# Three moves in a fused attention, mixture-of-experts and channel-mix kernel: when one expert's rows are loaded, where weight words are decoded, and where they are checked

## The chip, the core and the metric

The kernel runs on one core of a Trainium2 chip. TensorE (PE) does the matmuls, VectorE (DVE), ScalarE (ACT) and GpSimd (POOL) the rest, each working through its own list of instructions in order; SyncE (SP) issues most loads. Sixteen DMA engines move data between HBM and the on-chip memory. The metric is the device time of one execution in microseconds (us), as the median of several runs.

## The reference, cut to what matters

Three stages follow each other on 2 x 768 tokens of width 512. The second and third are

```python
# attention output x, (2, 768, 512), goes into
for b in range(B):
    for s in range(S):
        e = fresh_e if s == 0 or local_gate[b, s] < 0.5 else prev_e   # one of 8 experts
        h = np.maximum(x[b, s] @ w1[e], 0.0)                            # 512 -> 1024
        out[b, s] = p[e] * (h @ w2[e])                                  # 1024 -> 512
...
x_prev = np.concatenate([np.zeros((B, 1, D)), x[:, :-1, :]], axis=1)
xk = mu_k * x + (1.0 - mu_k) * x_prev
xr = mu_r * x + (1.0 - mu_r) * x_prev
k = np.maximum(xk @ w_k, 0.0)          # w_k (512, 1024), float64 in memory
v = k * k @ w_v                        # w_v (1024, 512), float64 in memory
r = 1.0 / (1.0 + np.exp(-(xr @ w_r)))  # w_r (512, 512), float64 in memory
return r * v
```

The three matrices of the last stage arrive as 64-bit numbers, so each is a pair of 32-bit words on the chip.

## The kernel before

**Matmuls in three.** Each float32 product is three matmuls (`mm3`, L608 to L610): every operand is split into a rounded "hi" part, made by an ACT copy, and a "lo" rest, made by a subtraction on DVE. So each tile of weights (512 KB) is loaded into one of four `wraw` buffers by SP, turned into `whi` by ACT (L596, two halves) and into `wlo` by DVE (L605). The buffer is free when `wlo` is made; `w_lo_all` is followed by `pump`, which issues the next load of the queue `lq` on SP. Activations go the same way (`xh`/`xl`, `hh`/`hl`, `ehh`/`ehl`).

**Stages by time.** Attention and routing take about 0 to 136 us; the routing sorts the tokens by expert into a DRAM table `xs`. Experts are then worked by rank `r`, most tokens first. The rank 0 expert is done in part while routing ends (its steps are called `fill` steps), and its third tile of 128 rows follows from about 155 to 171 us (`xs_tile`). A branch `tc.If(more > 0)` comes next, whose body isn't run with this data. Then r=1 with three tiles of rows (171 to 206 us), r=2 (206 to 230), r=3 (230 to 246), r=4 (246 to 269), r=5 (269 to 285), r=6 (285 to 310) and r=7 (310 to 333). Ranks 3 and 5 have one tile of 128 rows and are done in the form of `xs_tile`: first layer into `hn`, four transposes of `hn` on PE (L614), split into `ehh`/`ehl`, second layer. Ranks 1, 2, 4 and 6 have a first layer of eight steps f (`l1m`) and a second layer (`l2_mm`) for each tile of rows. The results leave by `yo` (two buffers) and a DMA to `ys`.

**Rows of an expert.** `x_load(r)` reads the rows of rank r from `xs` into tiles `xn`. PE transposes them (`x_hi`, L1180), ACT and DVE split them. For r=1 the entry stands in `lq` ahead of its weights, and the transposes are spread over the third tile of rank 0.

**Decoding 64-bit words.** 15 pieces (`LATER`) of the last stage's weights are decoded on DVE, each with three instructions of 128x512 (`decode_fast`, L469, L471, L473). `B_(1)` runs one step of a generator; a piece has four steps, of which one emits nothing, so there are 60 steps. Each piece is loaded (`dw`, two buffers) by a DMA on POOL's queue, which is issued once the piece two before it is done. A table `BL1` says at which f of a first layer a step goes; in a second layer a step goes to every second f.

**Checking 64-bit words.** The kernel relies on no weight being tiny. `guard()` reads 20 further pieces (`g`, from SP, L1339, in the five `z` buffers) and keeps the smallest square of each (`smallest`, L462, a custom DVE instruction). A table `GUARD` puts the checks ahead of the steps f of the last stage.

**The last stage** has six blocks b of 256 tokens: eight `k_step`s (matmuls, ACT `rl`, DVE `sq`, then POOL `kl`), two `r_unit`s (the gate r), two `v_unit`s (the second matrix; each ends with DVE `o`). `prep` makes the next block's mixed input beside this (`xmk`, `xmr`, then `xkl`, `xrl` on DVE).

The order on each engine is as the code is written; no scheduler reorders it.

Of the kernel before, what the change touches and what calls it, by code (L numbers as in the profile page):

```python
# [16 lines left out]
P = 128  # L17
# [16 lines left out]
REG = B * S  # L34
# [517 lines left out]
def build(ctx, tc, ins, out):  # L552
# [277 lines left out]
    rsteps = []  # L830

# [74 lines left out]
    with tc.manual_schedule():  # L906
# [216 lines left out]
        w_load(1, 2)  # L1123
        w1q = [(c, s) for c in range(2) for s in range(4)]
        for k, _ in enumerate(fl):
            E_(1)
            if k > 6 and w1q:
                c, s = w1q.pop(0)
                if s < 2:
                    w_hi1(1, c, s)  # L1130
                else:
                    w_lo1(1, c, s - 2)
                if s == 3:
                    raws.pop((1, c))
                    if c == 0:
                        w_load(1, 3)
# [5 lines left out]
    xn, xhl, hs, xps, h3 = {}, {}, {}, {}, {}  # L1142
# [292 lines left out]
    def stage3():  # L1435
        for b in range(NB):
# [10 lines left out]
            if b == 1:  # L1447
                gd = guard()
                for i in range(3):
                    g_load(i)  # L1450
            if b == NB - 1:
                small = n.small_w3(rp)
            for f in range(KF):
                if f in GUARD[b]:
                    next(gd)
                if b == NB - 1 and f in (5, 7):
                    next(small)
                if f in (1, 2) and a:
                    scale(2 * b + 1 + f)
                k_step(b, f)  # L1460
                if f:
                    k_split(b, f - 1)
                if a:
                    a.pop(0)()
                if b == 0:
                    W_(2)
            k_split(b, KF - 1)
            if b:
                for i in range(2):
                    r_unit(b, i)  # L1470
                    if a:
                        a.pop(0)()
            for i in range(2):
                v_unit(b, i)
                for _ in range(2):
                    if l:
                        l.pop(0)()
# [3 lines left out]
    GUARD = ((), (5, 7), (0, 2, 4, 5, 7), (0, 2, 4, 5, 7), (0, 2, 4, 5, 7), (0, 2, 4))  # L1481
    DVEHI = (4, 5, 6, 7)
    BL1 = (1, 1, 1, 0, 1, 1, 1, 1)
# [7 lines left out]
    with tc.manual_schedule():  # L1491
        lq = []

        for r in range(1, E):
            if r == 1:
                lq.append(lambda r=r: x_load(r))
            else:
                lq.append(lambda r=r: ereg(r))
# [39 lines left out]
        pump(3)  # L1538
# [15 lines left out]
        for r in range(1, E - 1):  # L1554
# [12 lines left out]
            for f in range(KF):  # L1567
# [6 lines left out]
                B_(BL1[f])  # L1574
            nt = len(TILES[r])
            for i in range(nt):
# [6 lines left out]
                for f in l2_mm(r, ps, a, src, m):  # L1583
                    W_(W2[nt][i][f])
                    if f % 2 == 0:
                        B_(1)
                    elif r > 1:
                        next(lr, None)
# [232 lines left out]
```

## Time and profile before

| | before |
|---|---|
| time, median of 3 runs | 521.37 us (520.94 to 525.34) |
| the profiled execution's own time | 520.07 us |
| its span | 518.3 us |
| PE busy in the span | 490.4 us (95%) |
| DVE busy | 355.5 us (69%) |
| ACT busy | 257.5 us (50%) |
| POOL busy | 127.6 us (25%) |
| mean granted clock of PE | 0.987 of full speed |

The profiled execution lies 1.3 us under the median of the runs. A span starts with the first instruction and ends with the last; a duration in a row is that of one execution.

### The profile page before, as it was taken

The page shows a single profiled execution, that of the slowest core. Times are in us where ns is not written, and L with a number is a line of the kernel's source. Part 1 is how long each engine was busy: PE and PEld are TensorE (multiplying, and loading weights), DVE is VectorE, ACT ScalarE, POOL GpSimd, SP SyncE. Part 2 cuts the span into 40 slices and gives each one's busy share as a digit, 9 for nine tenths or more (in the row PEclk, how much of TensorE's full clock was granted, in tenths as well). Part 3 has the DMA queues.
Part 4 walks back from the last instruction along what each step waited for, and adds up shares of the span by engine and source line. Part 5 has one row for each costly group of instructions (what it writes and reads, how often), then busy time and mean ns, then how long its engine had stood idle before and what let it go on. Part 6 is the DMA issues. An engine that isn't in the chain of part 4 may idle for free.

```text
span 518.3 us, 9357 instructions
## 1 busy us (share of the span) xinstructions
PE 490.4 (95%) x3191; PEld 411.2 (79%) x3191; DVE 355.5 (69%) x897; ACT 257.5 (50%) x629; POOL 127.6 (25%) x224
## 2 busy tenths in 40 slices
PE   8899998979898999998998999999999999999995
PEld 5688776767686877976986988788988989898985
DVE  7677886986785577986986963698465838375511
ACT  4766676753345355648647663674341414243220
POOL 6012112642100000010000000526281817344220
PEclk9899999999999999999998999999999999999998
DMA  8965655841657838897896851111514325250101
GB/s 177 231 181 151 159 147 132 270 164 41 244 223 240 303 122 266 336 326 275 300 334 230 298 189 38 44 61 53 205 59 127 129 87 197 61 193 32 40 4 46
DMA packets 76874, 86.99 MB, mean 168 GB/s; under 512 B 50928, under 2 KB 51184, under 8 KB 76816
## 3 DMA queue, kind: packets, MB, share of 16 engines
q1 hardware_dynamic: 68896, 65.41, 40.0%
q0 software_dynamic: 4080, 14.16, 8.3%
q10 hardware_dynamic: 3840, 6.72, 3.4%
q8 instruction: 28, 0.46, 0.4%
q14 instruction: 30, 0.25, 0.1%
HBM read 73.26 MB, written 13.01 MB: 166 GB/s over the span
## 4 chain that ended last, share of the span: by engine, by line
PE 64%; DVE 19%; DMA 7%; ACT 5%; issue 3%; SPq 0%; POOL 0%; ACTq 0%; DVEq 0%; POOLq 0%
PE O L608 7%; PE O L610 7%; PE O L609 7%; PE S L608 6%; PE S L609 6%; PE S L610 6%; DMA wraw<-in_moe_w_dram 4%; DVE wlo L605 4%; PE O L814 4%; PE S L756 4%; PE PT L608 2%; PE PT L610 2%; PE PT L609 2%; PE PT L788 2%; DVE zt L769 2%
## 5 line engine op out<-in xcount | busy, mean ns | idle before, releaser
L596 ACT ACTIVATE whi<-wraw 128x512 fp32r<-128x512 f32 x116 | 67.1, 624 | 29.5 <-DMA wraw<-in_moe_w_dram 27.6
L605 DVE TENSOR_TENSOR wlo<-wraw,whi 128x1024 fp32r<-128x1024 f32 x54 | 65.6, 1218 | 12.4 <-ACT whi L596 11.8
L1358 ACT ACTIVATE rl<-S 128x256 f32<-128x256 f32 x48 | 18.5, 385 | 82.2 <-PE S L610 82.2
L608 PE MATMUL S<-xkh,whi 128*128 128x256 f32 x192 | 55.4, 288 | 0.4 <-DVE sq L1360 0.3
L609 PE MATMUL S<-xkl,whi 128*128 128x256 f32 x192 | 54.0, 281 | 0.6 <-DVE xkl L1323 0.6
L610 PE MATMUL S<-xkh,wlo 128*128 128x256 f32 x192 | 54.0, 281 | 0.0
L1368 POOL TENSOR_TENSOR kl<-sq,kh 128x256 fp32r<-128x256 f32 x40 | 34.1, 861 | 76.4 <-ACT kh L1367 76.4
L779 ACT ACTIVATE peb<-zt,nm 128x232 f32<-128x232 f32 (+1 forms) x96 | 44.2, 464 | 10.9 <-PE PT L790 4.0
L1398 DVE TENSOR_TENSOR o<-O,sig 128x512 f32<-128x512 f32 (+1 forms) x13 | 8.5, 651 | 58.4 <-PE O L610 34.8
L608 PE MATMUL O<-whi,kh 128*128 128x512 f32 (+1 forms) x104 | 39.6, 380 | 0.0
L610 PE MATMUL O<-whi,kl 128*128 128x512 f32 (+1 forms) x104 | 39.2, 377 | 0.0
L609 PE MATMUL O<-wlo,kh 128*128 128x512 f32 (+1 forms) x104 | 39.0, 375 | 0.0
L608 PEld LDWEIGHTS S<-xkh,whi 128*128 128x128 f32 x192 | 36.3, 189 | 1.8 <-DVE sq L1360 1.5
L609 PEld LDWEIGHTS S<-xkl,whi 128*128 128x128 f32 x192 | 36.3, 189 | 1.0 <-DVE xkl L1323 0.8
L769 DVE CUSTOM_DVE_ANT_0 zt<-S,tb 128x232 f32<-128x232 f32 (+1 forms) x94 | 30.3, 375 | 9.3 <-PE S L756 7.8
L610 PEld LDWEIGHTS S<-xkh,wlo 128*128 128x128 f32 x192 | 36.2, 189 | 0.0
L1360 DVE SCALAR_TENSOR_TENSOR sq<-S,rl 128x256 f32<-128x256 f32 x48 | 20.1, 418 | 14.2 <-ACT rl L1358 13.7
L788 PE MATMUL PT<-ident,peb 128*128 128x128 f32 x96 | 23.7, 287 | 4.0 <-DVE RI L187 1.9
L608 PE MATMUL O<-whi,hh 128*128 128x512 f32 x64 | 25.6, 400 | 0.1
L268 POOL DMA_INDIRECT xs<-X,posi x12 | 13.0, 1079 | 51.3 <-DMA xs<-X,posi 11.6
L610 PE MATMUL O<-whi,hl 128*128 128x512 f32 x64 | 25.3, 395 | 0.0
L609 PE MATMUL O<-wlo,hh 128*128 128x512 f32 x64 | 25.1, 393 | 0.0
(351 smaller groups left out, 1380.2 us busy)
## 6 DMA issues: line engine op xcount, KB each, us to landing
wraw<-in_moe_w_dram SPq DMA_DIRECT2D x64, 512.0 KB, 4.9
dw<-in_moe_w_v_dram POOLq DMA_DIRECT2D x8, 512.0 KB, 5.9
g<-in_moe_w_k_dram SPq DMA_DIRECT2D x8, 512.0 KB, 8.7
g<-in_moe_w_v_dram SPq DMA_DIRECT2D x8, 512.0 KB, 4.2
ys<-yo ACTq DMA_DIRECT2D x15, 256.0 KB, 4.1
dw<-in_moe_w_k_dram POOLq DMA_DIRECT2D x7, 512.0 KB, 7.3
vn<-in_v_dram SPq DMA_DIRECT2D x12, 256.0 KB, 4.5
xn<-xs SPq DMA_DIRECT2D x12, 256.0 KB, 4.5
```

The lines of the kernel that those rows point to most:

```text
L596: nc.scalar.activation(out=whl[r, c][0][:, sl], in_=raws[r, c][:, sl], func=ACTF.Copy)
L605: nc.vector.tensor_tensor(lo, raws.pop((r, c)), hi.bitcast(F32), op=ALU.subtract)
L608: nc.tensor.matmul(out_, lhsT=ah, rhs=bh, start=first, stop=False)
L609: nc.tensor.matmul(out_, lhsT=ah, rhs=bl, start=False, stop=False)
L610: nc.tensor.matmul(out_, lhsT=al, rhs=bh, start=False, stop=last)
L756: nc.tensor.matmul(ps[a], lhsT=qz[t % 2][a * HD:(a + 1) * HD, p, :], rhs=strip[a * HD:(a + 1) * HD, p, k0:k0 + N], start=True, stop=True)
L769: nc.vector.tensor_tensor_reduce(out=sc[:, c0:W], in0=ps[a], in1=(n.tb if t % NT else n.tb0)[:, h + a, :], scale=1.0, scalar=3.0e38, op0=A ...
L779: nc.scalar.activation(out=pe[:, PAD + c0:2 * P], in_=sc[:, c0:W], func=ACTF.Exp, scale=-1.0, bias=nm[:, h + a:h + a + 1], accum_out=sm[:, ...
L788: nc.tensor.transpose(ps[:, a * P:(a + 1) * P], pe[:, P:2 * P], n.ident)
L814: nc.tensor.matmul(Os[t][a * HD:(a + 1) * HD, p * P:(p + 1) * P], lhsT=v_src(t, c)[:, (h + a) * HD:(h + a + 1) * HD], rhs=pt[:, (2 * c + a ...
L1360: nc.vector.scalar_tensor_tensor(sq_, ps[:, 0:TB], 0.0, rl, op0=ALU.max, op1=ALU.mult)
L1368: (nc.gpsimd if b else nc.vector).tensor_tensor(hl, sq_, hh.bitcast(F32), op=ALU.subtract)
```

## The change

It has three parts.

A. The rank 1 expert's rows are loaded in the fill, right behind the rows `x0` of the third tile of rank 0, into a `wraw` buffer (`xa`, two tiles of rows) and a `yo` buffer (`xb`, 80 rows), where before they went into `xn` tiles later. The weight tiles 2 and 3 of rank 1 are issued after tiles 0 and 1 have been split.

B. The decode steps are spread in another way. Steps by place, before and after: third tile of rank 0: 8 and 8; r=1: 7+12 and 4+12 (first layer + second layer); r=2: 7+8 and 0+4; r=4: 7+8 and 0+8; r=6: 3 (what was left) and 4+8; r=7: 0 and 12.

C. The checks leave the `k_step`s. Blocks 1 to 4 have five each: one after each `r_unit`, two behind them, and one between the two `v_unit`s. Block 5 has none.

```diff
@@ build, behind the ranks @@
         nc.sync.dma_start(out=x0, in_=n.xs[bass.ds(row, P), :])
-        w_load(1, 2)
+        xa = wp.tile([P, 2, D], F32, tag="wraw", bufs=4, name="xa")
+        for i, t in enumerate((xa[:, 0, :], xa[:, 1, :], rp.tile([P, D], F32, tag="yo", bufs=2, name="xb"))):
+            m = LAST if i == 2 else P
+            row = nc.values_load(n.rowi[:, i, 1:2], engines=(SP,), min_val=0, max_val=E * REG - m)
+            nc.sync.dma_start(out=t[0:m, :], in_=n.xs[bass.ds(row, m), :])
+            xn[1, i] = t
...
                 if s == 3:
                     raws.pop((1, c))
-                    if c == 0:
-                        w_load(1, 3)
+                    w_load(1, c + 2)
@@ stage3 @@
+        gd = guard()
+
+        def guards(b, m):
+            for _ in range(m if 0 < b < NB - 1 else 0):
+                next(gd)
...
-                if f in GUARD[b]:
-                    next(gd)
...
                     r_unit(b, i)
                     if a:
                         a.pop(0)()
+                    guards(b, 1)
+            guards(b, 2)
             for i in range(2):
+                if i:
+                    guards(b, 1)
                 v_unit(b, i)
...
-    GUARD = ((), (5, 7), (0, 2, 4, 5, 7), (0, 2, 4, 5, 7), (0, 2, 4, 5, 7), (0, 2, 4))
-    BL1 = (1, 1, 1, 0, 1, 1, 1, 1)
+    BL1 = {1: (0, 1, 0, 1, 0, 1, 0, 1), 2: (0,) * 8, 4: (0,) * 8, 6: (0, 1, 0, 1, 0, 1, 0, 1)}
...
         for r in range(1, E):
-            if r == 1:
-                lq.append(lambda r=r: x_load(r))
-            else:
+            if r > 1:
                 lq.append(lambda r=r: ereg(r))
...
-        pump(3)
+        pump(2)
...
-                B_(BL1[f])
+                B_(BL1[r][f])
...
-                    if f % 2 == 0:
+                    if f % (4 if r == 2 else 2) == 0:
                         B_(1)
-                    elif r > 1:
+                    if f % 2 and r > 1:
                         next(lr, None)
```

**SP, where the fill ends.** A name like `wraw1_2` is weight tile 2 of rank 1; an ISA row waits or sets a register. Before:

```order
94 L1122 DMA x0_2037<-xs_63 128x512
95 L568 ISA
96 L568 DMA wraw1_2_2049<-in_moe_w1_dram 128x1024
97 L568 ISA
98 L568 DMA wraw1_3_2126<-in_moe_w1_dram 128x1024
99 L1165 TENSOR_LOAD rowi_2009
100 L1165 ISA x2
101 L1167 ISA
102 L1167 DMA xn1_0_2187<-xs_63 128x512
```

After, where `x0` and the first half of `xa` stand right ahead of this piece:

```order
102 L1128 DMA xa_2049<-xs_63 128x512
103 L1127 TENSOR_LOAD rowi_2009
104 L1127 ISA x2
105 L1128 ISA
106 L1128 DMA xb_2050<-xs_63 80x512
107 L568 ISA
108 L568 DMA wraw1_2_2159<-in_moe_w1_dram 128x1024
109 L568 ISA
110 L568 DMA wraw1_3_2189<-in_moe_w1_dram 128x1024
```

The three loads of rank 1's rows have moved ahead of weight tiles 2 and 3.

**DVE, second half of the first layer of r=4.** `hl4_f` is the rest of hidden step f, `w3_k<-dw` a decode instruction, `wlo5_c` the rest of weight tile c of rank 5. Before:

```order
600 L605 TENSOR_TENSOR wlo5_0_3681<-wraw5_0_3561,whi5_0_3680 128x1024
601 L471 SCALAR_TENSOR_TENSOR w3_6_3641<-dw12_3387,w3_6_3641 128x512
602 L1205 SCALAR_TENSOR_TENSOR hl4_6_3710<-PT_258_3711,hh4_6_3709 128x256
603 L473 SCALAR_TENSOR_TENSOR w3_6_3641<-dw12_3387,w3_6_3641 128x512
604 L1205 SCALAR_TENSOR_TENSOR hl4_7_3729<-PT_259_3730,hh4_7_3728 128x256
605 L605 TENSOR_TENSOR wlo5_1_3706<-wraw5_1_3563,whi5_1_3705 128x1024
606 L469 TENSOR_SCALAR w3_6_3641<-dw13_3639 128x512
607 L605 TENSOR_TENSOR wlo5_2_3755<-wraw5_2_3565,whi5_2_3754 128x1024
608 L404 SCALAR_TENSOR_TENSOR t8_3787<-OH_287,iota_e_103 128x96
609 L405 TENSOR_REDUCE pf_3788<-t8_3787 128x12
610 L471 SCALAR_TENSOR_TENSOR w3_6_3641<-dw13_3639,w3_6_3641 128x512
611 L605 TENSOR_TENSOR wlo5_3_3795<-wraw5_3_3607,whi5_3_3794 128x1024
```

After:

```order
587 L605 TENSOR_TENSOR wlo5_0_3655<-wraw5_0_3540,whi5_0_3654 128x1024
588 L1210 SCALAR_TENSOR_TENSOR hl4_6_3682<-PT_258_3683,hh4_6_3681 128x256
589 L1210 SCALAR_TENSOR_TENSOR hl4_7_3700<-PT_259_3701,hh4_7_3699 128x256
590 L605 TENSOR_TENSOR wlo5_1_3679<-wraw5_1_3542,whi5_1_3678 128x1024
591 L605 TENSOR_TENSOR wlo5_2_3724<-wraw5_2_3544,whi5_2_3723 128x1024
592 L404 SCALAR_TENSOR_TENSOR t8_3758<-OH_287,iota_e_103 128x96
593 L405 TENSOR_REDUCE pf_3759<-t8_3758 128x12
594 L469 TENSOR_SCALAR w3_4_3729<-dw8_3237 128x512
595 L605 TENSOR_TENSOR wlo5_3_3766<-wraw5_3_3585,whi5_3_3765 128x1024
```

Four decode instructions between `wlo5_0` and `wlo5_3` have become one. In the same way r=2 has none left between `hl2_0` and `wlo3_3`, where it had seven.

**DVE, second layer of r=6 into r=7.** `ehl0` is the rest of rank 7's hidden activations of its first tile, in two halves. Before, the two halves have no decode instruction ahead of them:

```order
674 L605 TENSOR_TENSOR wlo7_7_4348<-wraw7_7_4275,whi7_7_4347 128x1024
675 L617 TENSOR_TENSOR ehl0_4363<-PT_283_4388,ehh0_4362 128x512
676 L601 TENSOR_TENSOR wlo8_8_4383<-w3_8_2057,whi8_8_4382 128x512 x2
677 L617 TENSOR_TENSOR ehl0_4363<-PT_285_4415,ehh0_4362 128x512
678 L601 TENSOR_TENSOR wlo8_9_4410<-w3_9_2106,whi8_9_4409 128x512 x2
```

After:

```order
664 L473 SCALAR_TENSOR_TENSOR w3_6_4308<-dw12_4245,w3_6_4308 128x512
665 L605 TENSOR_TENSOR wlo7_7_4332<-wraw7_7_4251,whi7_7_4331 128x1024
666 L469 TENSOR_SCALAR w3_6_4308<-dw13_4306 128x512
667 L471 SCALAR_TENSOR_TENSOR w3_6_4308<-dw13_4306,w3_6_4308 128x512
668 L473 SCALAR_TENSOR_TENSOR w3_6_4308<-dw13_4306,w3_6_4308 128x512
669 L617 TENSOR_TENSOR ehl0_4348<-PT_283_4381,ehh0_4347 128x512
670 L469 TENSOR_SCALAR w3_7_4377<-dw14_4353 128x512
671 L601 TENSOR_TENSOR wlo8_8_4373<-w3_8_2090,whi8_8_4372 128x512 x2
672 L471 SCALAR_TENSOR_TENSOR w3_7_4377<-dw14_4353,w3_7_4377 128x512
673 L473 SCALAR_TENSOR_TENSOR w3_7_4377<-dw14_4353,w3_7_4377 128x512
674 L617 TENSOR_TENSOR ehl0_4348<-PT_285_4411,ehh0_4347 128x512
```

Pieces 13 and 14 now stand ahead of the two halves. The checks of part C: in before, between two blocks, DVE has `o`, `xrl`, a check and `sq(b,0)`; in after it has four checks ahead of the first `o`, one between `xkl` and the second `o`, and `xrl` is followed by `sq(b,0)`.

## Rows read from the trace of the kernel before

**Rows 1.** First part of the page: PE's busy time, its share of the span, instructions.

```profile
PE 490.4 (95%) x3191; PEld 411.2 (79%) x3191; DVE 355.5 (69%) x897; ACT 257.5 (50%) x629; POOL 127.6 (25%) x224
```

**Rows 2.** What PE waited for: us in total, times, longest us.

```profile
PE PT L614 <- ACT hn L626: 3.8, 2, 2.1
...
PE T L1180 <- DMA xn<-xs: 2.1, 1, 2.1
...
PE PT L608 <- DVE h3l L1205: 0.8, 2, 0.4
```

**Rows 3.** PE in order of time, 159.5 to 170: start us, us, instruction, idle before.

```profile
161.03 0.40 PE L609 MATMUL S<-wlo,x0s 128*128 128x512 f32 x1
161.26 0.40 PE L610 MATMUL S<-whi,x0s 128*128 128x512 f32 x1
163.72 0.66 PE L1180 MATMUL T<-ident,xn 128*128 128x128 f32 x4 [2.07 <-DMA xn<-xs]
```

**Rows 4.** The chain that ended last, 150 to 172: start us, us, what.

```profile
158.03 8.30 DMA xn<-xs
...
171.83 6.67 DMA ys<-yo
```

**Rows 5.** The chain that ended last, whole span, in ranks 2 and 4.

```profile
227.79 5.56 DMA wraw<-in_moe_w_dram
...
264.34 7.14 DMA wraw<-in_moe_w_dram
```

**Rows 6.** PE in order of time, 272 to 279.5.

```profile
275.37 0.91 PE L614 MATMUL PT<-ident,hn 128*128 128x128 f32 x4 [2.15 <-ACT hn L626]
...
277.36 0.63 PE L608 MATMUL S<-whi,xh 128*128 128x512 f32 x1
277.79 0.63 PE L609 MATMUL S<-wlo,xh 128*128 128x512 f32 x1
```

**Rows 7.** Stretches of 10 us: busy time by engine, PEclk, DMA share, GB/s.

```profile
220.00:230.00 10.00, 10.00 (x43) 7.71 (x42) 9.69 (x29) 5.26 (x10) 1.06 (x2) 1.00 0.87 292
...
270.00:280.00 10.00, 7.85 (x32) 6.07 (x31) 6.79 (x13) 5.99 (x12) 0.00 (x0) 0.83 0.89 323
...
310.00:320.00 10.00, 10.00 (x49) 8.13 (x48) 4.81 (x7) 5.53 (x11) 0.10 (x1) 1.00 0.07 26
```

**Rows 8.** The tile dw: durations in ns (minimum, median, maximum), and landings.

```profile
L469 DVE TENSOR_SCALAR w<-dw x15: 404/419/461, 167.9 to 288.6; 128x512 uint32<-128x512 uint32 x15
L471 DVE SCALAR_TENSOR_TENSOR w<-dw,w x15: 672/683/693, 169.4 to 291.3; 128x512 uint32<-128x512 uint32 x15
...
DMA to landing us min/median/max: 4.1/6.8/9.6
```

**Rows 9.** DVE and ACT in order of time, end of r=6 and first tile of r=7.

```profile
309.42 1.16 ACT L596 ACTIVATE whi<-wraw 128x512 fp32r<-128x512 f32 x2 [1.81 <-DMA wraw<-in_moe_w_dram]
...
312.61 0.60 ACT L626 ACTIVATE hn<-S 128x512 f32<-128x512 f32 x1 [1.54 <-PE S L610]
...
315.07 0.69 DVE L617 TENSOR_TENSOR ehl<-PT,ehh 128x512 fp32r<-128x512 f32 x1 [3.24 <-ACT ehh L616]
...
318.31 0.69 DVE L617 TENSOR_TENSOR ehl<-PT,ehh 128x512 fp32r<-128x512 f32 x1 [1.34 <-ACT ehh L616]
```

**Rows 10.** The chain that ended last, 421 to 430, from block 2 to 3.

```profile
424.90 0.69 DVE o L1398
...
426.73 0.60 DVE g L462
```

**Rows 11.** PE in order of time at the same place.

```profile
427.41 0.28 PE L610 MATMUL S<-xkh,wlo 128*128 128x256 f32 x1
427.73 0.38 PE L608 MATMUL S<-xkh,whi 128*128 128x256 f32 x1
```

**Rows 12.** DVE in order of time, 400 to 420: the idle time ahead of the first `o`.

```profile
419.36 0.69 DVE L1398 TENSOR_TENSOR o<-O,sig 128x512 f32<-128x512 f32 x1 [5.88 <-issue]
```

**Rows 13.** Loads of weight tiles on the page: KB each, median us to landing.

```profile
wraw<-in_moe_w_dram SPq DMA_DIRECT2D x64, 512.0 KB, 4.9
```

More of the change, by code (lines that the diff above doesn't have):

```diff
@@ L830, in build @@
     rsteps = []
+    xn = {}
     def early_start():
@@ L1141, in build @@
     mp = mstack.enter_context(tc.tile_pool(name="mp", bufs=1))
-    xn, xhl, hs, xps, h3 = {}, {}, {}, {}, {}
+    xhl, hs, xps, h3 = {}, {}, {}, {}
     TILES = [(2,)] + [(0, 1, 2)] + [(0,) if r in SHORT else (0, 1) for r in range(2, E)]
@@ L1447, in stage3 @@
             if b == 1:
-                gd = guard()
                 for i in range(3):
```

## The prediction

> **What bounds the kernel now.** The page's first part comes first: PE is busy 490.4 us of 518.3 [rows 1], so only what makes PE wait is worth anything, at most some tens of us. The next view is the list of what PE waited for [rows 2]. A reader is to see that its first line is a wait for `hn`, an ACT result, 3.8 us in two places, and that rank 1's rows (`xn`) cost a wait of 2.1 us. The third view is PE in order of time at these places [rows 3, 6], which shows how long PE really stood still, and the fourth the chain that ended last [rows 4, 5], which tells what was late behind the engine named.
>
> At r=3 and r=5 the chain reads: DVE works without a break up to the `wlo` that frees a `wraw` buffer, then the load into that buffer takes 5.56 us and 7.14 us [rows 5]. ACT stands in order before that tile's `whi`; `hn` is queued behind it. DVE was busy 9.69 of 10 us ahead of the first of these [rows 7]. So `hn` is late because the last weight load was issued late and landed slowly; ACT itself is not the cause. The second gap has a sequel: the granted clock falls to 0.83 over the stretch 270 to 280 [rows 7], and for some eight matmuls the distance from start to start is 0.43 us (277.36 to 277.79) [rows 6], where the same shape has 0.23 (161.03 to 161.26) [rows 3]. That is the lower level, 1.2 GHz, after PE had stood still for 2.15 us; at the first gap, of 1.64 us, the clock did not fall.
>
> In the last stage PE has no listed wait worth naming. But between blocks the chain runs through DVE: `o` at 424.90, then `xrl`, then a check `g` at 426.73 of 0.60 us, then `sq` [rows 10], and PE's next matmul starts 0.32 us after the one before, where the step is 0.12 [rows 11]. With a second, smaller slip behind it this is 0.3 us a boundary, at four boundaries.
>
> **The change part by part.**
>
> **A, the rows of rank 1.** Removed is the wait for a transfer of 8.30 us [rows 4]; PE's start-to-start distance was 163.72 - 161.26 = 2.46 for a step of 0.23 [rows 3], so 2.2 us, and 0.2 more at the third tile of rows. The rows now go out right behind `x0`, some 15 us earlier, and the tables that they read are complete by then, as for `x0`. The three DMAs are the same, only earlier. SP issues weight tiles 2 and 3 of rank 1 behind them: tile 3 now takes the buffer that `wlo1_1` frees, at about 156 us where it was 147, and would land 4.9 us later [rows 13], near 161, for a first layer that starts at 171. The cover is those 10 us; a slip beyond it would show as a wait for `whi` at 171. Rank 1's tile 5 takes `xa`'s buffer after its transposes, at about 162, which is where it was. What is late next is `hn`/`ehl` of the same tile, on DVE, by less than 0.5. Gain 0.5 to 2.4; I take 2.0, near the wait itself.
>
> **B, the decode steps.** A decode instruction costs 0.42 or 0.68 us [rows 8]. In r=4 the part of DVE's list from `wlo5_0` to `wlo5_3` loses 0.68 + 0.68 + 0.42 + 0.68 and keeps 0.42: 2.0 us less DVE work ahead of the release of the buffer of tile 7 (three more are gone earlier in that layer). In r=2 all seven between `hl2_0` and `wlo3_3` are gone, about 4 us. If the release comes earlier by that, the `hn` gaps of 1.64 and 2.15 us, 3.8 together, go. The limit is that the `hl` in between wait for PE itself, so that DVE cannot run ahead at will. Bounds 0 and 3.8; I take 3.0, nearer to full closing, since the DVE relief is about as large as either gap. The clock's sequel is eight matmuls at 0.20 us more, 1.6 us; it goes if the second gap becomes clearly shorter than the first gap's 1.64, where the clock stayed: 1.3, bounds 0 and 1.6. Of the wait for `h3l` in r=1, 0.8 us [rows 2], where three of seven steps go: 0.4, bounds 0 and 0.8.
>
> How far the loads themselves get faster is a second question. The `dw` and the weight loads overlap in those stretches, in which the DMA share is 0.87 and 0.89 [rows 7], and the late tile took 7.14 us where the median is 4.9 [rows 5, 13]. The Trainium skill, "DMA: Bandwidth & Descriptors", section "Issuing engines are not separate DMA queues", says that transfers started by different engines run on the same 16 DMA engines and interleave. By that rule the `dw` loads that leave r=4 shorten the weight loads too, and both gaps close in full, 3.8 instead of 3.0; without it only the DVE relief counts.
>
> What B adds lies later. In r=6 there are 12 steps for 3. Four instructions of them (0.42 + 0.68 + 0.68 + 0.42 = 2.2 us) stand ahead of `wlo7_3`, which frees the buffer of tile 7 of rank 7; some of it fills DVE's idle time there, so I take 0.9 of delay (0 to 2.2). ACT then waited 1.54 us for PE before `hn` of r=7 [rows 9]: 0.9 is covered, 2.2 would show 0.7. In r=7 itself, piece 13 (0.42 + 0.68 + 0.68 = 1.8) lies in the idle 3.24 us ahead of the first `ehl`; piece 14, as long, is put ahead of the second, where the idle time was 1.34 [rows 9]: 0.4 late. In addition the load of piece 14 goes out only when piece 12 is done, at about 310.5, beside `whi` of 309.42; it lands 4.1 to 9.6 us later [rows 8], from 314.6 to 320.1, and is wanted at 315.8. Behind a decode that waits for it are queued `wlo8_8` and the second `ehl`, and PE waits for that `ehl`. The DMA share there is only 0.07 [rows 7], so I go near the lower end. Cost of r=7: 0.6, bounds 0 and 4.
>
> **C, the checks.** The check leaves the chain at the four boundaries: 4 x 0.3 = 1.2; I take 1.0, bounds 0 and 1.2, as `xrl` still stands there. Its new places are covered: four checks of about 0.7 us fall into an idle time of DVE of 5.88 ahead of `o` [rows 12], and the fifth into the wait for the second `o`. If that cover is gone, `o` comes late and the bank of the next `v_unit` with it, but by 2 us there is room. The checks' loads on SP come in bursts now; the DMA engines have room there, and the output DMAs are not waited for.
>
> **Sum.** 2.0 + 3.0 + 1.3 + 0.4 + 1.0 - 0.6 = 7.1. Against the profiled execution's own time: 520.07 - 7.1 = 513.0. That execution lies 1.3 under the median of 521.37, so the forecast for the median is **514** (rounded from 514.3).
>
> **The rivals.**
>
> *Loads are the bound, not DVE.* The DMA share of 0.87 to 0.89 speaks for it, and that a load of 5 to 7 us stands in the chain. Against it: DVE's list decides when the load is issued, and the `dw` loads leave as well. Then the gaps at r=3 and r=5 stay with their clock, and only A and C come: 520.07 - 3.0 + 0.6 = 517.7, median 519.
>
> *Slower: the decode of r=7 waits for its loads.* The same condition taken further: a `dw` load takes its longest, 9.6 us [rows 8], also where the DMA engines are idle. Piece 13, issued near 306.5, lands at 316, and the first `ehl` ends at 318.5, where 315.8 was wanted: 2.7. Piece 14 lands at 320.1; its other instructions and `wlo8_8` follow before the second `ehl`, near 323.5 for 319.0: 1.8 more. Piece 15 goes out near 317.8, lands at 327.4, and holds the first `ehl` of the second tile (315.07 + 12 = 327.1 before) by some 2; a clock that falls after such a stop costs 1.6 again. That is 8. With the gaps at r=3 and r=5 left as they are, 520.07 - 3.0 + 8 = 525, median 526. It decides from a landing of about 7 us on. The median of 6.8 speaks for it, the DMA share of 0.07 against it.
>
> *Rank 1's rows come in time and nothing is won.* After the branch ACT stands for 6.67 us behind the DMA of `yo` [rows 4]. If its end hangs on something that does not move with PE, the first layer of r=1 waits longer, and of A 0.5 is left: 513.0 + 1.5 = 514.5, median 516.
>
> *The change does not take the check out of the chain.* If the slip between blocks is `o` and `xrl` alone, C is worth nothing: 514.0, median 515.3.
>
> **How the numbers follow.** Forecast 0.52, loads as the bound 0.24, rows without gain 0.10, checks without gain 0.07, slower by r=7 0.07. The range reaches down to the sum of the upper bounds, 2.4 + 3.8 + 1.6 + 0.8 + 1.2 = 9.8, or 511.6 and a little for waits too small to be listed: 510.5. Upward it takes in the loads' rival, 519.5. A change of 1% is 5.2 us, about what a measurement of this kernel can tell from none. Faster by over 1% means under 516.2: nearly all of the forecast, seven tenths of the rival without gain from the rows, most of that of the checks, 0.60 together. Slower by over 1% is the r=7 rival, 0.06; the rest is 0.34.
>
> **What would show it.** The transposes of rank 1's rows start without idle time ahead of them. The list of PE's waits no longer begins with `hn`, the load ahead of r=5 is issued two us earlier relative to PE, and the clock of that stretch is 1.00. Between blocks, `xrl` is followed by `sq` on DVE and PE's step there is under 0.2. In r=7, decode rows show little idle time put down to a `dw` DMA. The prediction is wrong if `hn` still leads the waits, if r=7's second `ehl` comes over a us later than PE wants it, or if a wait for `whi1_3` stands at the start of r=1.

## The result, and the profile after

The changed kernel takes 514.36 us (median of 4 runs, 512.22 to 515.85), against 521.15 us for the kernel before in the same comparison. The ratio is 0.9859 with a 95% interval of 0.9816 to 0.9902. Timed a second time (e9, below) it gave 514.49 us and 0.9870 (0.9835 to 0.9906). The profiled execution is the slowest of the first four, 515.85 us with a span of 514.1 and a clock of 0.992, so the two traces are compared stretch by stretch and not by their ends.

What PE waited for in the changed kernel; the columns are those of [rows 2]:

```profile
PE PT L788 <- DVE RI L187: 1.8, 3, 1.3
PE R L236 <- DVE ab L226: 1.6, 2, 1.2
...
PE S L608 <- DVE hl L1210: 1.0, 1, 1.0
PE O L610 <- DVE ehl L617: 0.7, 2, 0.5
```

The two lines that the prediction started from, `hn` and `xn`, are gone from the list. The first two lines lie in attention and routing, which are the same in both kernels. Longer than before or new are a wait for `hl` of 1.0 us, which stands in the first layer of r=2, and two for `ehl`. Further down the list has a wait for `whi` of 0.6 us at the start of r=1, which the prediction named as a sign of being wrong. It is no new wait: PE stood 0.56 us at that place before as well, under the name of the branch (`PEq L1551`).

PE in order of time at the transposes of rank 1's second tile of rows, which answers to [rows 3]:

```profile
162.59 0.39 PE L610 MATMUL S<-whi,x0s 128*128 128x512 f32 x1
162.81 0.60 PE L1185 MATMUL T<-ident,xa 128*128 128x128 f32 x4
```

The distance from start to start is 0.22 us where it was 2.46. ACT in order of time around the branch shows what part A moved in exchange:

```profile
167.72 1.16 ACT L596 ACTIVATE whi<-wraw 128x512 fp32r<-128x512 f32 x2 [0.47 <-DMA wraw<-in_moe_w_dram]
169.39 1.15 ACT L596 ACTIVATE whi<-wraw 128x512 fp32r<-128x512 f32 x2 [0.51 <-DMA wraw<-in_moe_w_dram]
170.45 0.58 ACT L657 ACTIVATE yo<-O 128x512 f32<-128x512 f32 x1
171.06 0.33 ACTq L658 DMA_DIRECT2D ys<-yo  x1
178.38 0.39 ACT L1209 ACTIVATE hh<-S 128x256 fp32r<-128x256 f32 x1 [7.35 <-issue]
```

These are weight tiles 4 and 5 of rank 1, then `yo`, then ACT's stop at the branch, then the first hidden step of r=1. The two pairs of `whi` copies now wait for their loads, and `yo` comes behind them without any idle time of its own. In the kernel before the same copies ran in one piece, and ACT then waited for PE ahead of `yo`:

```profile
167.59 2.71 ACT L596 ACTIVATE whi<-wraw 128x512 fp32r<-128x512 f32 x5
171.20 0.60 ACT L657 ACTIVATE yo<-O 128x512 f32<-128x512 f32 x1 [0.90 <-PE O L610]
```

At r=5 PE's idle time at the place of [rows 6] fell from 2.15 us to 0.10, and the clock did not fall. From start to start it is 0.50 us, where 0.23 is the usual step. PE in order of time, and the stretch that answers to [rows 7]:

```profile
271.51 0.40 PE L610 MATMUL S<-whi,xl 128*128 128x512 f32 x1
272.01 0.66 PE L614 MATMUL PT<-ident,hn 128*128 128x128 f32 x4
```

```profile
270.00:280.00 10.00, 9.44 (x48) 6.94 (x47) 6.44 (x13) 8.04 (x16) 0.04 (x1) 1.00 0.92 358
```

Between blocks 2 and 3, DVE in order of time shows four checks ahead of the first `o`, one between the `o`s, and `xrl` followed by `sq`, which answers to [rows 10]:

```profile
409.35 1.23 DVE L462 CUSTOM_DVE_ANT_0 g<-g 128x512 f32<-128x512 f32 x1
...
411.73 0.69 DVE L462 CUSTOM_DVE_ANT_0 g<-g 128x512 f32<-128x512 f32 x1
...
416.15 0.69 DVE L1403 TENSOR_TENSOR o<-O,sig 128x512 f32<-128x512 f32 x1 [3.74 <-issue]
...
422.30 1.22 DVE L1328 TENSOR_TENSOR xrl<-xmr,xrh 128x1024 fp32r<-128x1024 f32 x1
423.58 0.42 DVE L1365 SCALAR_TENSOR_TENSOR sq<-S,rl 128x256 f32<-128x256 f32 x1
```

The idle time ahead of `o` fell from 5.88 [rows 12] to 3.74 and was not used up. PE keeps its step of 0.12 us there (424.20 to 424.31 and on), where [rows 11] have 0.32.

In r=7, DVE in order of time has the waits that the prediction was afraid of, only small ones:

```profile
311.53 0.68 DVE L617 TENSOR_TENSOR ehl<-PT,ehh 128x512 fp32r<-128x512 f32 x1
312.67 0.43 DVE L469 TENSOR_SCALAR w<-dw 128x512 uint32<-128x512 uint32 x1 [0.46 <-DMA dw<-in_moe_w_v_dram]
313.02 1.29 DVE L601 TENSOR_TENSOR wlo<-w,whi 128x512 fp32r<-128x512 f32 x2
314.22 0.68 DVE L471 SCALAR_TENSOR_TENSOR w<-dw,w 128x512 uint32<-128x512 uint32 x1
314.94 0.69 DVE L473 SCALAR_TENSOR_TENSOR w<-dw,w 128x512 uint32<-128x512 uint32 x1
315.55 0.68 DVE L617 TENSOR_TENSOR ehl<-PT,ehh 128x512 fp32r<-128x512 f32 x1
```

Between the two halves of `ehl` DVE is idle for 0.46 us only, waiting for piece 14, and PE waits 0.51 us for the second half. In a second profile of the same kernel (e9, below) DVE waits 1.42 us there and PE 1.47.

**Where the time went.** The table is made from PE in order of time: a stretch runs from the first matmul with the weights of one rank to the first with those of the next; the third tile of rank 0 from its first matmul with its own rows; the last column from the first `sq` of block 1 to that of block 5. r=4 and r=6 stayed within 0.2 us in all runs and are left out. One profiled execution each, in us.

| run | third tile of rank 0 | r=1 | r=2 | r=3 | r=5 | r=7 | blocks 1 to 5 |
|---|---|---|---|---|---|---|---|
| before | 16.65 | 34.51 | 24.26 | 14.91 | 16.88 | 25.72 | 117.70 |
| changed | 14.38 | 35.50 | 24.66 | 13.21 | 14.24 | 26.81 | 116.26 |
| e1, part A | 14.36 | 35.63 | 24.93 | 14.67 | 18.00 | 25.71 | 117.66 |
| e2, part B | 17.23 | 35.03 | 24.67 | 13.04 | 13.96 | 27.42 | 117.70 |
| e3, part C | 16.47 | 34.45 | 24.48 | 17.87 | 17.17 | 25.75 | 116.25 |
| e4, r=1's steps kept | 14.36 | 34.90 | 23.99 | 13.05 | 15.01 | 27.61 | 116.26 |
| e5, before with fewer dw loads | 17.42 | 34.42 | 24.42 | 13.29 | 14.59 | 25.77 | 117.56 |
| e6, before with light decode | 18.68 | 34.50 | 24.52 | 14.22 | 17.17 | 25.76 | 117.72 |
| e7, changed, r=7 without loads | 14.41 | 35.39 | 24.59 | 13.04 | 14.04 | 26.02 | 116.25 |
| e8, changed, tile 5 behind branch | 14.35 | 35.62 | 24.19 | 13.05 | 13.87 | 28.07 | 116.26 |
| e9, changed again | 14.37 | 35.59 | 24.28 | 13.05 | 13.93 | 27.67 | 116.25 |
| e10, steps in r=5 | 14.36 | 35.06 | 24.16 | 13.06 | 14.58 | 26.02 | 116.25 |
| e11, none in r=7 | 14.37 | 35.08 | 24.50 | 13.04 | 14.44 | 26.11 | 116.25 |
| e12, all moves | 14.35 | 34.65 | 24.49 | 13.04 | 14.25 | 25.85 | 116.25 |

From before to changed: -2.27, +0.99, +0.40, -1.70, -2.64, +1.09, -1.44, together -5.6 us. The ends of the spans differ by 4.2 only, since the changed kernel's profiled execution reached the third tile 1.4 us later. The start of that tile lies between 153.0 and 156.6 us in the fourteen executions, with part A and without.

### The profile page after: what moved, and what is told of

The parts are those of the page before. It is cut to its first block, busy times and chain, and to the rows that moved or that the text cites. A ratio compares the mean times of both kernels' runs of the same rounds, so it can differ in the third digit from the quotient of the medians.

```text
span 514.1 us, 9352 instructions
## 1 busy us (share of the span) xinstructions
PE 491.2 (96%) x3191; PEld 410.8 (80%) x3191; DVE 352.4 (69%) x897; ACT 258.2 (50%) x629; POOL 123.9 (24%) x224
## 4 chain that ended last, share of the span: by engine, by line
PE 59%; issue 20%; DVE 11%; DMA 5%; ACT 4%; POOL 1%; ACTq 0%; SPq 0%; POOLq 0%; DVEq 0%
PE S L608 6%; PE S L610 6%; PE S L609 6%; PE O L608 5%; PE O L610 5%; PE O L609 5%; PE S L756 4%; PE O L814 4%; DMA dw<-in_moe_w_v_dram 2%; PE PT L788 2%; PE PT L608 2%; PE PT L610 2%; PE PT L609 2%; DVE zt L769 2%; PE R L196 2%
## 5 line engine op out<-in xcount | busy, mean ns | idle before, releaser
L1373 POOL TENSOR_TENSOR kl<-sq,kh 128x256 fp32r<-128x256 f32 x40 | 32.0, 808 | 78.2 <-ACT kh L1372 78.2
L1250 POOL DMA_DIRECT2D dw<-in_moe_w_v_dram x8 | 4.2, 530 | 101.5 <-DVE w L473 101.5
L756 PE MATMUL S<-strip,zt 64*128 64x232 f32 (+1 forms) x188 | 25.6, 393 | 0.0
```

What stands on the lines that cost most here:

```text
L756: nc.tensor.matmul(ps[a], lhsT=qz[t % 2][a * HD:(a + 1) * HD, p, :], rhs=strip[a * HD:(a + 1) * HD, p, k0:k0 + N], start=True, stop=True)
L1373: (nc.gpsimd if b else nc.vector).tensor_tensor(hl, sq_, hh.bitcast(F32), op=ALU.subtract)
```

## The experiments

The kernels of one group below (e1 to e4, e5 to e8, e9 to e12) ran on the same chip beside the same runs of the kernel before. In the first group its median was 521.27 us, in the second 522.28, in the third 521.93.

**e1, e2, e3: each part alone.** The edits are the three parts of the diff that is shown ahead of the prediction, one at a time.

Part A:

> Part A alone (rank 1's rows early), the rest as before. My account: the wait ahead of the transposes of rank 1's second tile of rows is gone, 2.2 to 2.5 us of PE time between the end of the fill and the branch; nothing else moves, time 2 to 2.5 us under before (ratio 0.995 to 0.996). Rival (the gain is handed back behind the branch, where ACT stands for 7 us): the wait is gone but the first results of r=1 come no earlier relative to the fill, time within 0.5 us of before.

Measured: 517.63 us, ratio 0.9928 (0.9895 to 0.9961). The wait ahead of the transposes is gone: the third tile takes 14.36 us. But r=1 takes 35.63 us for 34.51 and r=2 24.93 for 24.26. ACT in order of time, with the same rows as above:

```profile
166.72 1.16 ACT L596 ACTIVATE whi<-wraw 128x512 fp32r<-128x512 f32 x2 [1.55 <-DMA wraw<-in_moe_w_dram]
168.05 1.16 ACT L596 ACTIVATE whi<-wraw 128x512 fp32r<-128x512 f32 x2 [0.18 <-DMA wraw<-in_moe_w_dram]
169.11 0.57 ACT L657 ACTIVATE yo<-O 128x512 f32<-128x512 f32 x1
...
177.01 0.38 ACT L1209 ACTIVATE hh<-S 128x256 fp32r<-128x256 f32 x1 [7.33 <-PE PT L610]
```

SP issued weight tiles 4 and 5 of rank 1 7.7 and 7.0 us ahead of r=1's first matmul (161.03 and 161.68, to 168.72); before they went out 13.1 and 9.9 us ahead (158.63 and 161.79, to 171.72). `yo` comes 0.9 us later relative to PE, and the first `hh` of r=1 1.1 us later: 177.01 - 168.72 = 8.29, for 178.88 - 171.72 = 7.16. Both theories are half right: 2.3 us are won, and 1.1 of them are handed back in r=1. The time gained, 3.6 us, is more than the stretches of this one execution show; it was 519.52 us, well above its own median, with a gap of 3.28 us at r=5 that part A doesn't touch.

Part B:

> Part B alone (decode steps spread), the rest as before. My account: the two gaps of PE ahead of hn at r=3 and r=5 (1.6 and 2.2 us) and the low clock behind the second (1.6 us) go, 4.5 to 5.5 us; 1 to 1.5 us come back, as DVE waits for a dw load at the end of r=1 with hl of r=2 queued behind, and 0.5 to 1 us in r=7; net 2.5 to 4 us under before. Rival (the loads set the gaps and DVE does not): the gaps stay at over 1 us each and the time is that of before or above it.

Measured: 517.42 us, ratio 0.9927 (0.9899 to 0.9956), 3.8 us less. r=3 got shorter by 1.87 and r=5 by 2.92; r=1 and r=2 got longer by 0.5 and 0.4, and r=7 by 1.7. My account held in its numbers, and r=7 cost more than I had said. The rival isn't refuted by this: part B takes the dw loads away from the ends of r=2 and r=4 together with the decode, so this run can't tell the two apart.

Part C:

> Part C alone (checks moved out of the k_steps), the rest as before. My account: the four slips of 0.3 us between blocks go, 1.2 us, no new wait of PE in the last stage; time 1.0 to 1.2 us under before. Rival (o and xrl hold sq up anyway): slips of 0.2 to 0.3 us stay between blocks and the time is that of before.

Measured: 520.52 us, ratio 1.0018 (0.9973 to 1.0063): the time alone can't tell. The blocks can: 116.25 us for 117.70. This value is the same to 0.01 us in every kernel with part C, and 117.56 to 117.72 in every kernel without it. So C is worth 1.45 us. This execution had a gap of 3.16 us at r=3, which C doesn't touch either: with the decode steps where they were, these gaps differ from one execution to the next.

**e4: more steps in r=1.** In the changed kernel:

```diff
-    BL1 = {1: (0, 1, 0, 1, 0, 1, 0, 1), 2: (0,) * 8, ...
+    BL1 = {1: (1, 1, 1, 0, 1, 1, 1, 1), 2: (0,) * 8, ...
```

> The changed kernel with seven decode steps kept in the first layer of r=1, as before, in place of four; r=7 gets nine for twelve. My account: the loads of pieces 5 and 6 go out some 6 us earlier, DVE's wait of 3.3 us for piece 6 at the end of r=1 falls to under 1.5 us and PE's wait of 1.0 us for hl of r=2 goes; r=7 loses its wait of 0.5 us: 1 to 1.5 us under the changed kernel, 511 to 513 if that stands at 513 to 514. Rival (that wait is set by the weight loads that crowd the DMA engines there, whatever the order): it stays, and the first layer of r=1 gains waits for h3l of 0.3 us: same time as the changed kernel or 0.5 us more.

Measured: 514.56 us, the changed kernel's time, where I had expected 511 to 513. PE's wait for `hl` at r=2 fell from 0.98 to 0.32 us, and r=1 and r=2 lost 0.6 and 0.7 us, as I had said. But all later pieces moved up by three steps. The gap at r=5 came back, 1.15 us, and r=7 cost 0.8 more. DVE's work in r=4 was the same eight steps, but one of their instructions now stands ahead of the `wlo` that frees the buffer of tile 6 of rank 5. DVE in order of time in e4, around the `wlo` of tiles 1 and 2:

```profile
256.02 1.22 DVE L605 TENSOR_TENSOR wlo<-wraw,whi 128x1024 fp32r<-128x1024 f32 x1
257.15 0.69 DVE L473 SCALAR_TENSOR_TENSOR w<-dw,w 128x512 uint32<-128x512 uint32 x1
257.75 1.22 DVE L605 TENSOR_TENSOR wlo<-wraw,whi 128x1024 fp32r<-128x1024 f32 x1
```

In the changed kernel the two follow each other:

```profile
257.31 2.35 DVE L605 TENSOR_TENSOR wlo<-wraw,whi 128x1024 fp32r<-128x1024 f32 x2
```

In e4 the loads of tiles 6 and 7 go out 0.6 us later relative to r=5's first matmul: tile 7 4.36 us ahead of it for 4.96. From its issue to its first use it takes 6.0 us for 5.6. A dw load went out 8.1 us ahead of r=5's first matmul, where the changed kernel has its first at 2.9 ahead. So of the 1.0 us by which tile 7 is late, 0.6 is the decode instruction and 0.4 the slower load.

**e5 and e6: the decode's loads or its DVE time.** Both edit the kernel before, for pieces 8 to 15 only. e5 leaves the loads out and keeps the decode:

```diff
+            t = dw[i]
             yield from dec(i)
             for j in LATER[k_ + 2:k_ + 3]:
-                dec_load(j)
+                if k_ < 5:
+                    dec_load(j)
+                else:
+                    dw[j] = t
```

> The kernel before with its last eight loads of 64-bit words dropped (pieces 8 to 15 decode the seventh tile's words again, so the last matrices are other numbers): the DMA work of r=2 to r=4 falls by 8 x 512 KB, DVE's list is unchanged. My account (DVE's list issues the last weight load late, and the dw loads only slow its landing): the gaps ahead of hn at r=3 and r=5 shrink but stay, about 1 us each, as the load ahead of r=5 lands in 5 us for 7; 1 to 3 us under before. Rival (the DMA engines are the bound): both gaps go to under 0.3 us and the low clock with them, 4 to 5.5 us under before.

e6 keeps the loads and cuts the decode:

```diff
         nc.vector.tensor_scalar(d, hi, 3, 0x3FFFFFF8, ...)
+        lo, hi, d = lo[:, 0:n], hi[:, 0:n], d[:, 0:n]      # n = 16 for pieces 8 to 15
         yield
```

> The kernel before with the second and third decode instruction of pieces 8 to 15 cut to 16 of 512 columns (the decoded words lack their sign and low bits): DVE is freed of 1.1 to 1.2 us a piece in r=2 to r=4, all loads and all waits stay in their places. My account: the release of the last buffer comes 1.5 to 2 us earlier, the gaps of 1.6 and 2.2 us fall to under 0.6 each and the low clock goes: 3 to 5 us under before. Rival (the DMA engines are the bound): the gaps stay at over 1 us each, as the loads land when the queue lets them, and the time is within 1.5 us of before.

Measured: e5 515.43 us, ratio 0.9880 (0.9815 to 0.9946); e6 517.28 us, ratio 0.9894 (0.9817 to 0.9970). The times overlap, the traces do not. In e5 the gap at r=3 is gone (13.29 us) and the one at r=5 is 1.43 us with no fall of the clock (14.59). In e6 r=3 keeps 0.77 us (14.22), and r=5 has 2.42 us, with the low clock behind it (17.17). The load of rank 5's last tile shows the difference; SP and POOL are in the rows of issues, ACT's `whi` is the first use. In e5, from SP's and ACT's rows in order of time:

```profile
262.50 0.38 SPq L570 DMA_DIRECT2D wraw<-in_moe_w_dram  x1
```

```profile
268.31 1.15 ACT L596 ACTIVATE whi<-wraw 128x512 fp32r<-128x512 f32 x2 [2.90 <-DMA wraw<-in_moe_w_dram]
```

In e6, whose line numbers are higher by one:

```profile
264.34 0.53 POOL L1246 DMA_DIRECT2D dw<-in_moe_w_v_dram  x1 [5.06 <-DVE w L474]
264.96 0.38 SPq L571 DMA_DIRECT2D wraw<-in_moe_w_dram  x1
```

```profile
272.60 1.15 ACT L597 ACTIVATE whi<-wraw 128x512 fp32r<-128x512 f32 x2 [4.16 <-PE S L611]
```

The last bracket names PE, but the load itself landed at 272.50, 0.1 us ahead of the copy. In the changed kernel:

```profile
262.59 0.38 SPq L570 DMA_DIRECT2D wraw<-in_moe_w_dram  x1
```

```profile
268.22 1.16 ACT L596 ACTIVATE whi<-wraw 128x512 fp32r<-128x512 f32 x2 [2.64 <-DMA wraw<-in_moe_w_dram]
```

When the last tile is ready depends on two things: when its load goes out, counted back from the rank's first matmul (the lead), and how long it takes from there to `whi`. The table has both, with PE's idle time ahead of the transposes of `hn` (the gap), all in us:

| run | r=3: lead | to `whi` | gap | r=5: lead | to `whi` | gap |
|---|---|---|---|---|---|---|
| before | 4.81 | 7.13 | 1.64 | 4.52 | 7.25 | 2.15 |
| e5, before with fewer dw loads | 4.79 | 5.49 | 0 | 3.80 | 5.82 | 1.43 |
| e6, before with light decode | 5.47 | 6.92 | 0.77 | 4.63 | 7.64 | 2.42 |
| changed | 5.82 | 6.44 | 0 | 4.96 | 5.63 | 0.10 |

A dw load close to the last weight load makes that load slower. At r=5 it took 7.15 to 7.64 us to `whi` in the four profiles with a dw load issued within 0.7 us of it (before, e1, e3, e6), and 5.19 to 6.02 in the other ten. The DVE time sets the lead. At r=3 it is 0.7 us longer with the light decode and 1.0 longer in the changed kernel. At r=5 of e5, where no dw load flies, 1.43 us of the gap are left: the load takes about as long as in the changed kernel, but goes out 1.16 us later. So at r=3 the rival is right in e5, and at r=5 my account is; neither cause alone explains both gaps. From before to changed, the last tile of rank 3 is ready 1.7 us earlier, 1.0 by the lead and 0.7 by the faster load; that of rank 5 2.05 us earlier, 0.43 by the lead and 1.62 by the faster load.

e6 doesn't isolate the DVE time at r=5, since its decode also finished earlier and sent the next dw load out ahead of the weight load, and one decode instruction stayed ahead of the `wlo` of tile 2. Its profile is also the slowest of four runs, 521.15 us, while two of the others took 514.1 and 514.4; their gaps are not known.

The rows of SP show why the lead at r=5 grew so little. In all fourteen profiles the last tile's load goes out 2.9 us behind that of tile 6, and SP works on the two loads of the next rank's rows in between (before: 261.45, then 262.61 and 263.74, then 264.34). The buffer that `wlo5_3` frees was ready by then (263.61 before). What counts is the `wlo` of tile 2, which lets tile 6 go; decode instructions behind it did not delay this load.

**e7: r=7 without its loads.** In the changed kernel, with the same edit as e5 for pieces 13 to 15.

> The changed kernel without the loads of pieces 13 to 15, which are decoded in r=7 from the words of piece 12 (the last matrix is another): DVE's list in r=7 is unchanged, but waits for no load. If the 1.1 us that r=7 lost is a wait of the decode for its loads, with ehl behind it, the stretch of r=7 falls from 26.8 to 25.7 to 25.9 us and PE waits for ehl under 0.2 us. If it is the decode's own DVE time, it stays at 26.3 to 26.8 and PE's wait for ehl stays at 0.4 us or more.

Measured: 512.24 us, ratio 0.9819 (0.9751 to 0.9886). r=7 takes 26.02 us for 26.81 in the first profile of the changed kernel and 27.67 in the second, and PE's one listed wait for `ehl` is 0.2 us. So 0.8 to 1.65 of the loss is the wait for the loads. The 0.3 that is left (26.02 to 25.72) is probably the decode's own DVE time, which no run tests by itself.

**e8: tile 5 behind the branch.** In the changed kernel:

```diff
-    W0 = (0, 0, 0, 0, 0, 0, 0, 1, 2, 1, 2, 1, 2, 1, 1, 1)
+    W0 = (0, 0, 0, 0, 0, 0, 0, 1, 2, 1, 2, 1, 2, 0, 0, 0)
...
-   W_((...)[f] if r == 2 else (1, 2, 2, 1, 2, 2, 1, 1)[f])
+   W_((...)[f] if r == 2 else (4 if r == 1 else 1, 2, 2, 1, 2, 2, 1, 1)[f])
```

> The changed kernel with the split of rank 1's weight tile 5 moved behind the branch (the first step of r=1's first layer), so that yo of the third tile of rank 0 does not stand behind a whi that waits for its load. My account of what part A hands back (whi of tiles 4 and 5 wait for loads that now go out some 1.4 us later, yo and ACT's stop at the branch come later, so hh of r=1): hh1_0 comes 7.0 to 7.2 us after the first matmul of r=1 in place of 7.6, and the stretch of r=1 falls from 35.5 by 0.5 to 34.9 to 35.0 us; time 0 to 0.5 us under the changed kernel. Rival (ACT's return does not hang on yo): hh1_0 stays at 7.5 or later and r=1 gets longer by 0.3 to 1 us, as tile 5 is split when ACT is busiest.

Measured: 513.40 us, ratio 0.9847 (0.9793 to 0.9902). The first `hh` of r=1 comes 6.26 us after r=1's first matmul, earlier than I had said, and still r=1 takes 35.62 us: three `whi` copies stood between the first and the second `hh`, 2.57 us apart for 1.53. The gain was spent at once. That ACT's return hangs on `yo` is not shown: `yo` starts 0.52 us ahead of r=1's first matmul here as in e10 below, and e10 has its first `hh` at 7.71. r=7 had its longest wait for a dw load, 28.07 us.

**e9 to e12: the changed kernel again, and three versions of it.** e9 is the changed kernel:

> The changed kernel itself, timed again beside the next three. Both theories: the median stands at 513 to 515, and the profile's stretches repeat: r=1 35.4 to 35.6 us, r=2 24.6, r=3 13.0 to 13.3, r=5 13.9 to 14.3, r=7 26.5 to 27.5.

It gave 514.49 us, ratio 0.9870 (0.9835 to 0.9906), and its stretches repeated but for r=2, 24.28 for 24.6, and r=7, 27.67.

e10 keeps the dw loads away from the end of r=4, and puts four steps at the end of r=5:

```diff
-    BL1 = {1: (0, 1, 0, 1, 0, 1, 0, 1), 2: (0,) * 8, ...
+    BL1 = {1: (1, 1, 1, 0, 1, 1, 1, 1), 2: (0,) * 8, ...
...
                     W_(WS[u])
+                    B_(1 if r == 5 and u > 11 else 0)
...
-                    if f % (4 if r == 2 else 2) == 0:
+                    if f % (4 if r == 2 else 2) == 0 or (r, i, f) == (2, 1, 6):
```

> The changed kernel with seven decode steps in the first layer of r=1, five in the second layer of r=2, four at the end of r=5, and so four in r=7 for twelve. Account that fits the runs so far (a dw load that flies together with the last weight load of an expert makes it land late; in r=7 the decode waits for dw loads that go out too late): r=7 falls from 26.8 to 25.9 us, r=1 and r=2 by 0.6 each, r=3 and r=5 stay at 13.0 to 14.3, as no dw load is issued 4 to 10 us ahead of r=5's start: 2 us under the changed kernel. Rival (DVE's load decides): r=5 and r=6 get longer by the four steps, 1 us or more, and the time is that of the changed kernel or above.

Measured: 511.41 us, ratio 0.9800 (0.9762 to 0.9839), 3.1 us under e9. Of these its stretches account for 1.65, as its profiled execution also reached the third tile 1.5 us earlier. r=7 is 26.02, r=1 0.5 shorter, r=3 13.06, all as the account of the loads has it. r=5 is 14.58, 0.65 more than in e9, with a wait of PE for `ehh` of 1.0 us, for 0.5 in e9: that is the four steps' own price. r=2 is 24.16, for 24.66 and 24.28 in the two profiles of the changed kernel.

e11 adds `6: (1,) * 8` in `BL1`, so that r=7 has no step:

> The version before this with eight decode steps in the first layer of r=6 in place of four, so none is left for r=7. The account of the dw loads: r=7 stands at 25.7 us, and r=6 stays at 23.8 to 24.0, since hn of r=7 had 1.5 us of room in the kernel before: 0 to 0.3 us under the version before this. Rival (DVE in r=6 is full, at 9.7 of 10 us in the changed kernel): wlo of rank 7 comes late, hn of r=7 with it, and r=7's first gap is 0.5 to 2 us with a fall of the clock above 2 us: 0.5 to 3 us slower than the version before this.

Measured: 512.52 us, ratio 0.9822 (0.9781 to 0.9862); r=6 23.83, r=7 26.11. This is 1.1 us above e10, where I had expected 0 to 0.3 under it, though the intervals overlap. r=7 did not reach 25.7: with no step left in it, its transposes of `hn` start 0.3 us later after its first matmul than before (4.51 for 4.20). So the rival came about in small, 0.3 us without a fall of the clock.

e12 is e10 with the split of tile 5 behind the branch, spread over more steps of r=1 (`(1, 3, 3, 2, 2, 2, 1, 1)`):

> The version with four steps in r=5 and r=7, with the split of rank 1's tile 5 put behind the branch, three instructions spread over the steps f=1, 2 and 3 to 5 of r=1's first layer. If part A's give-back is ACT standing behind late weight loads ahead of the branch, hh1_0 comes 6.3 us after r=1's first matmul for 7.6 and, with less put between hh1_0 and hh1_1 than in the run with four at f=0, r=1 falls to 34.5 to 34.9 us: 0.3 to 1 us under the version with four steps in r=5. If r=1 is bound by ACT's backlog whatever comes first, r=1 stays at 34.9 or more and the time is that of the version with four steps in r=5.

Measured: 511.40 us, ratio 0.9800 (0.9766 to 0.9835). The first `hh` comes after 6.03 us and r=1 takes 34.65, so most of part A's give-back is recovered there; r=2, at 24.49 for 24.16, takes back some. The time is that of e10, so r=1's gain doesn't show in it. Both medians lie 10.5 us under the kernel before and 3.1 under the changed one.

## Why the prediction was right, point by point

The forecast of 514 us met 514.36, and the list of waits without `hn`, the clock of 1.00 behind r=5, the step between blocks and the waits in r=7 of the first profile were as said. Two signs did not come as said: the load ahead of r=5 went out 0.4 us earlier relative to PE and not two, and in the second profile (e9) r=7's second `ehl` came 1.47 us later than PE wanted it. That the sum is so near is in part luck. The stretches of the first two profiles give 5.6 us for the 7.1 of the sum, and the medians differ by 6.8. Part B's loss of 0.5 us in r=1 (35.03 in e2, for 34.4 to 34.5) was not foreseen, and C gave 0.45 more than said. The terms, each read from kernels with and without the part:

**A: said 2.0.** About right in sum, with a step missed. The wait itself was larger than in the one trace I had: 2.07, 3.07, 2.33, 3.32 and 2.94 us in the five profiled executions without part A, and the third tile fell from a mean of 17.3 us to 14.4. (The transfer of 8.30 us that I named is the one of the third tile of rows, whose wait was 0.24; the second tile's rows, issued at 156.50, were out for about 7.2.) What I missed is in "Rank 1's tile 5 takes `xa`'s buffer after its transposes, at about 162, which is where it was". I looked at when the buffer comes free on the clock, not relative to PE, and not at tile 4. Relative to r=1's first matmul both loads come later, tile 4 7.7 us ahead for 13.1 and tile 5 7.0 for 9.9, in e1 and the changed kernel alike, and their copies on ACT wait for them. The first `hh` of r=1 comes 7.05 to 7.15 us after r=1's first matmul without part A, 7.46 to 8.30 with it, and 6.0 to 6.3 where tile 5's split is behind the branch. So 0.5 us comes back in the changed kernel (35.50 for 35.03 in e2, which has the same decode steps), and 1.1 in e1. The rival of "rows without gain" named the right place and too large a price.

**B: said 3.0 + 1.3 + 0.4.** The gain at r=3 and r=5 is 1.7 + 2.6 us between the two first traces, 4.3 with the clock, as said; against e3 it is more, as its gaps were larger. The step that failed is its reason. I took the DVE relief as the cause "since the DVE relief is about as large as either gap", 2.0 us at r=5 and about 4 at r=3, and dw traffic as an addition. But the relief brought the last load forward by 0.4 and 1.0 us only. In both places DVE, freed of decode, then waits for `hh` from ACT (0.95 us at r=5), which is the limit that the prediction named and gave too little weight. And at r=5 the release by `wlo5_3`, which I counted, isn't what the load waits for, as SP is busy with the next rank's rows. The larger part, 0.7 + 1.6 us, is that the load lands faster. Two readings hid this: the 5.56 us in the chain at r=3 is the load of rank 4's first tile, and rank 3's last tile took 7.0 us (issued at 225.68, `whi` at 232.81), about as slow as at r=5.

The rule of the Trainium skill, "DMA: Bandwidth & Descriptors", section "Issuing engines are not separate DMA queues", that transfers started by different engines run on the same 16 DMA engines and interleave, was the better guide. The traces agree: at r=5 the weight load that SP issues took 5.2 to 6.0 us without a dw load from POOL close to it, and 7.2 to 7.6 with one. The rival "loads are the bound" had the larger cause; it went wrong in leaving the gaps in place, although the dw loads leave those stretches.

The clock's term came, but a gap's length alone doesn't decide it. PE stood 2.15 us at r=5 before and the clock fell, while at the third tile it stood 3.07 us in e2 and 3.32 in e5 and the clock stayed at 1.00. The 0.4 at `h3l` did not come: the list has 1.0 us in two waits after, for 0.8 before. In the first layer of r=2 there is a new wait, where DVE stood 3.29 us for a dw load that goes out later now (`hl` in the list of waits above).

**r=7: said 0.6 lost, bounds 0 and 4.** The mechanism was right, the size too small: 1.1 and 1.95 us in the two profiled executions of the changed kernel. The load of piece 14 landed 3.7 us after its issue in one of them (308.99 to 312.67) and 4.6 in the other, about as I took it, and DVE then had no slack: three instructions and `wlo8_8` stood ahead of the second `ehl` in any case. The slower rival did not come about, since the dw loads there took 3.7 to 4.7 us in these two.

**C: said 1.0.** It is 1.45: my 0.3 us a boundary counted the two largest slips, and there were 0.36 in all at each.

Whether the 3.6 us that e1 gained in time are all part A's stays open: its third tile, r=1 and r=2, against a mean of the runs with the same code there, give 2.9 - 1.1 - 0.5 = 1.3, and the interval of its ratio reaches down to 2.0.

## What to carry to other kernels

Ask for each critical load when it goes out, and what else is in flight beside it. Here another engine's load issued within 0.7 us of it cost 1.1 us or more, and at r=5 moving that load away was worth more than the DVE work taken out ahead of the issue (1.6 for 0.4 us); at r=3 it was the other way round (0.7 for 1.0). Read on the issuing engine whether the load really waits for the release that was made earlier. Where a step is spread to "free" places, follow its load as well: with two buffers, each piece's load goes out when the piece two before it ends, and the last pieces then wait for it in a place where no one has slack. And read when a buffer comes free relative to the engine that waits, not on the clock, when the change moves both.

## What the runs showed that was not expected

ACT stood still for 6 to 7.6 us at the branch whose body isn't run, in every kernel: 7.08 us before, 7.35 changed, 7.33 in e1, 6.18 in e8. The profile names a different releaser each time, among them none ("issue"). Its return doesn't follow its own arrival: `yo` starts 0.52 us ahead of r=1's first matmul before, in e8 and in e10, and the first `hh` comes 7.15, 6.26 and 7.71 us after it. The DMA packets of the traces point to something else. In all fourteen profiles a packet of 8 KB of the kind `instruction` ends 1.2 to 1.4 us ahead of that `hh` (before at 177.62 for 178.88, in e8 at 172.35 for 173.64, in e10 at 174.08 for 175.33). So ACT most likely waits for its own code there. No run tests this, and what sets the time of that packet stays open.

The same gap differs between executions of kernels with the same code there: at r=3 1.64, 1.42 and 3.16 us, and at r=5 2.15, 3.28 and 2.44 (before, e1, e3). The kernel before ran from 517.9 to 525.6 us in the eleven runs beside e5 to e8, the changed kernel from 512.2 to 516.5 in ten. The spread is smaller with the dw loads away from the critical loads; that this is the cause is not shown.
